# Memory features from the transposed queries, denominators from the memory's product, and one inversion of softmax sums per unit

## The chip, the core and the metric

The kernel runs on one core of a Trainium2 chip. The metric is the device time of one execution in microseconds; a median over executions is given. The engines are TensorE (PE, matrix products and, as PEld, the loading of their weights), VectorE (DVE), ScalarE (ACT), GpSimd (POOL) and SyncE (SP, which issues most DMAs). PE writes to PSUM banks; DVE and ACT read them.

## The reference

The program is a chain of three layers: attention with a compressive memory, then two feed-forward layers. Cut to what matters:

```python
B, H, S, D = 4, 8, 576, 64
local = softmax(causal(q @ k.T / sqrt(D))) @ v          # per batch and head
phi = lambda x: np.where(x > 0, x, np.exp(x) - 1.0) + 1.0
mem_ret = einsum('bhsd,bhde->bhse', phi(q), M_prev)
mem_norm = einsum('bhsd,bhd->bhs', phi(q), z_prev)[..., None] + 1e-06
g = 1 / (1 + exp(-beta))                                # per head
x = g * mem_ret / mem_norm + (1 - g) * local            # -> [2304, 512]
x = leaky_relu(x @ w1_in) @ w1_out                      # 512 -> 2048 -> 512
h = x @ w2_in
out = (h - tanh(h)) @ w2_out
```

All inputs are float64 outside the chip or float32 after a conversion that the kernel does itself: the feed-forward weights arrive as pairs of 32-bit words and are turned into float32 by integer operations on DVE.

## The kernel before, in words

**Units.** Attention is cut into 32 units, each for one batch and two heads (a pair, 128 rows of q and k transposed, 64 per head). A unit of kind A has query rows 0 to 255 (two tiles of 128) and 256 keys, a unit of kind B query rows 256 to 575 (tiles of 128, 128 and 64) and all 576 keys. The 16 A units come first, four per batch, then the 16 B units. Four units of one batch and kind give one x block of 256 rows; the 64 left-over rows of the four batches form a ninth block, R.

**A unit's work.** SP loads q and k transposed (`qk`), q once more in natural layout (`rq`), z broadcast to all partitions (`zb`), M of both heads into the diagonal blocks of a 128x128 tile (`mb`), and v. PE makes scores (L584, and L589 for the 64-row tile), DVE masks them and takes the negative maxima (L610), ACT takes the exponential with its sum (L630), DVE adds 1e-9, divides by 1-g and inverts (L637, L641: one pair of instructions per tile), the scaling of the rows goes to ACT, DVE or POOL (L647 to L651), PE transposes (L703), ACT or DVE copies out of PSUM (`e_out`), PE multiplies with v (L725) into the output bank `o`, and the result is copied to `x`.

**The memory part** runs on natural q: ACT makes relu and exp (L500, L503), DVE the features (L506) and, for each tile and head, a product with z that is summed into a denominator (L513, an instruction and the reading of its accumulator), its inverse (L519), its gate (L523) and the product with the features (L530). PE transposes the features (L547) into a score bank `s`, a copy brings them to `pT`, and one product with `mb` (L670) opens the accumulation in `o`, to which the value products add.

**The feed-forward layers.** Layer 1 works on a block of 256 rows: x is split into a high and a low part (`xs`, on ACT and DVE, L412 for the low part), 24 products per pair of weight tiles (L851, `up`), the activation and its split, 24 products down (L953). For the first four blocks it is done in two sweeps, the first with 4 of 16 weight tiles (96 products per block), the second with the rest. Layer 1's products are the filler of PE during attention. Layer 2 (L1089 to L1120) follows after all attention and layer 1. Each weight tile of layer 1 is converted in four steps on DVE (L786, L789, L794, L799) after one on ACT (L783), and split (a copy and L412).

**What sets the order.** A list scheduler in the kernel (class `Schedule`) writes each engine's instructions in a fixed order. Each piece of work has engines with costs, a priority (unit number plus an offset for loads, memory, scores, values; layer 1's PE work behind attention), tiles that it reads, writes and takes from rings (`RINGS`: three score banks `s`, two `mb`, two `qk`, one `xs`). When costs, pieces or rings change, the whole order changes. On the chip each engine runs its list in that order and waits where an operand is missing.

Of the kernel before, what the change touches and what calls it, by code (L numbers as in the profile page):

```python
# [244 lines left out]
def kernel(  # L245
# [44 lines left out]
    omg4 = const.tile([128, H // 2], F32, name="omg4")  # L290
    mbs = [const.tile([128, 128], F32, name=f"mb{i}") for i in range(RINGS["mb"])]
    gate = const.tile([128, H], F32, name="gate")
# [27 lines left out]
    nc.sync.dma_start(out=gate, in_=beta.partition_broadcast(128))  # L320
    nc.scalar.activation(out=gate, in_=gate, func=AF.Exp, scale=-1.0)
    nc.vector.tensor_scalar(out=gate, in0=gate, scalar1=1.0, scalar2=None, op0=ALU.add)
    nc.vector.reciprocal(out=gate, in_=gate)
    nc.vector.tensor_scalar(out=omg, in0=gate, scalar1=-1.0, scalar2=1.0, op0=ALU.mult, op1=ALU.add)

    nc.vector.tensor_scalar(out=omg, in0=omg, scalar1=1e-30, scalar2=None, op0=ALU.max)
    nc.vector.reciprocal(out=omg, in_=omg)
    for i in range(2):
        p = slice(64 * i, 64 * i + 64)
        nc.vector.tensor_copy(out=omg4[p], in_=omg[p].rearrange("p (h j) -> p h j", j=2)[:, :, i])  # L330
# [86 lines left out]
    class Unit:  # L417
# [14 lines left out]
        def declare(self, pr, prev):  # L432
# [15 lines left out]
            qk, rq, zb, mb, v_ = new("qk"), new("rq"), new("zb"), new("mb"), new("v" if kind == "B" else "va")  # L448
# [9 lines left out]
            def load_q(e):  # L458
                rq.tile = att.tile([128, 3, 2, 64], F32, name="rq", bufs=RINGS["rq"])
                for i, h in enumerate(heads):  # L460
                    nc.sync.dma_start(
                        out=rq.tile[:, 0:nq, i, :],
                        in_=q[b, h, q0 * 128:(q0 + nq) * 128, :].rearrange("(t p) d -> p t d", p=128))

            def load_mz(e):
                zb.tile = att.tile([128, 2, 64], F32, name="zb", bufs=RINGS["zb"])
                nc.sync.dma_start(
                    out=zb.tile.rearrange("p h d -> p (h d)"),
                    in_=z_prev[b, 2 * hp:2 * hp + 2, :].rearrange("h d -> (h d)").partition_broadcast(128))
                mb.tile = mbs[mb.seq % RINGS["mb"]]  # L470
                for i, h in enumerate(heads):
                    nc.sync.dma_start(
                        out=mb.tile[i * 64:(i + 1) * 64, i * 64:(i + 1) * 64], in_=m_prev[b, h, :, :])
# [13 lines left out]
            op([("sp", 1000)], load_q, alloc=[rq], lat=2300)  # L487
            op([("sp", 1500)], load_mz, alloc=[zb, mb], lat=2300)
# [4 lines left out]
            ph, dn = new("ph"), new("dnm")  # L493

            def flat(t):
                return t.rearrange("p t h d -> p (t h d)")[:, 0:nf]

            def phi_neg(e):
                ph.tile = att.tile([128, 3, 2, 64], F32, name="ph", bufs=RINGS["ph"])
                nc.scalar.activation(out=flat(ph.tile), in_=flat(rq.tile), func=AF.Relu, scale=-1.0)  # L500

            def phi_exp(e):
                nc.scalar.activation(out=flat(ph.tile), in_=flat(ph.tile), func=AF.Exp, scale=-1.0)  # L503

            def phi_max(e):
                nc.vector.scalar_tensor_tensor(  # L506
                    out=flat(ph.tile), in0=flat(rq.tile), scalar=1.0, in1=flat(ph.tile), op0=ALU.add, op1=ALU.max)

            def phi_den(e):
# [712 lines left out]
```

## Time and profile before

| | |
|---|---|
| median of 3 runs | 1075.63 us (1075.47 to 1076.9) |
| span of the profiled execution | 1076.9 us |
| PE busy | 1042.5 us, 97%, 7488 products |
| DVE busy | 754.0 us, 70%, 2049 instructions |
| ACT busy | 637.7 us, 59% |
| mean granted clock of TensorE | 0.989 |
| chain that ended last | PE 83%, DMA 6%, DVE 5%, ACT 4% |

The profiled execution's own time is its span, as long as the longest of the three runs. Busy times are those of the profiler: the instructions of one engine overlap at their ends, so a duration is longer than the step from one start to the next, and a busy PE is not a PE at its peak. A row of the timeline gives the start, the duration, the engine, the line, what is written and read, the shape and the count; what stands in brackets at its end is idle time before it, and who ended that. The attention units and layer 1 lie in the first 662 us or so, layer 2 in the rest.

### The profile page before, as it was taken

The page shows a single profiled execution, that of the slowest core. Times are in us where ns is not written, and L with a number is a line of the kernel's source. Part 1 is how long each engine was busy: PE and PEld are TensorE (multiplying, and loading weights), DVE is VectorE, ACT ScalarE, POOL GpSimd, SP SyncE. Part 2 cuts the span into 40 slices and gives each one's busy share as a digit, 9 for nine tenths or more (in the row PEclk, how much of TensorE's full clock was granted, in tenths as well). Part 3 has the DMA queues.
Part 4 walks back from the last instruction along what each step waited for, and adds up shares of the span by engine and source line. Part 5 has one row for each costly group of instructions (what it writes and reads, how often), then busy time and mean ns, then how long its engine had stood idle before and what let it go on. Part 6 is the DMA issues. An engine that isn't in the chain of part 4 may idle for free.

```text
span 1076.9 us, 20416 instructions
## 1 busy us (share of the span) xinstructions
PE 1042.5 (97%) x7488; PEld 918.8 (85%) x7488; DVE 754.0 (70%) x2049; ACT 637.7 (59%) x1357; POOL 100.3 (9%) x102
## 2 busy tenths in 40 slices
PE   4799999999999999999999999999999999999997
PEld 2477799778689978979999999999999999999996
DVE  6999999888677587664212366867777676777765
ACT  5889876777673277361101134766666666666664
POOL 0001000000000000000000000221222222222221
PEclk9699999999999999999999999999999999999999
DMA  7867763655644354243100055010101101010000
GB/s 223 250 177 222 225 203 107 159 153 153 183 141 137 119 165 147 89 132 102 40 2 21 10 158 186 1 41 1 40 2 39 40 1 40 1 40 20 1 20 20
DMA packets 116403, 102.52 MB, mean 95 GB/s; under 512 B 63824, under 2 KB 92496, under 8 KB 116304
## 3 DMA queue, kind: packets, MB, share of 16 engines
q1 hardware_dynamic: 115088, 99.91, 31.2%
q10 hardware_dynamic: 1216, 1.31, 0.4%
q8 instruction: 59, 0.97, 0.4%
q14 instruction: 40, 0.33, 0.1%
HBM read 78.65 MB, written 22.54 MB: 94 GB/s over the span
## 4 chain that ended last, share of the span: by engine, by line
PE 83%; DMA 6%; DVE 5%; ACT 4%; issue 1%; SPq 1%; DVEq 0%; ACTq 0%
PE up L851 36%; PE dn L1120 18%; PE dn L953 18%; PE s L703 3%; PE o L725 3%; PE s L584 3%; PE s L589 1%; PE o L670 1%; DMA cv<-in_moe_w_in_dram 1%; DMA qk<-in_qkt_dram 1%; ACT e L630 1%; DMA x2s<-g 1%; DMA w<-in_moe_w_in_dram 1%; DMA vs<-cv 1%; ACT e L647 1%
## 5 line engine op out<-in xcount | busy, mean ns | idle before, releaser
L851 PE MATMUL up<-xs,w 128*128 128x256 f32 x3456 | 454.6, 284 | 0.4 <-ACT g L930 0.4
L851 PEld LDWEIGHTS up<-xs,w 128*128 128x128 f32 x3456 | 434.1, 190 | 12.4 <-issue 5.6
L953 PE MATMUL dn<-gh,w 128*128 128x256 f32 x1152 | 160.1, 286 | 0.0
L953 PEld LDWEIGHTS dn<-gh,w 128*128 128x128 f32 x1152 | 146.0, 192 | 7.2 <-issue 6.5
L1097 DVE SCALAR_TENSOR_TENSOR gf<-u,w 128x512 f32<-128x512 f32 x72 | 85.8, 1192 | 83.4 <-ACT w L1094 83.4
L1120 PE MATMUL dn<-w,gh 128*128 128x512 f32 x568 | 143.2, 394 | 0.6 <-ACT gh L1107 0.6
L412 POOL TENSOR_TENSOR gl<-gf,gh 128x512 fp32r<-128x512 f32 x71 | 92.2, 1299 | 506.9 <-ACT gh L1107 503.3
L930 ACT ACTIVATE g<-up 128x512 f32<-128x512 f32 x72 | 42.9, 595 | 146.4 <-PE up L851 138.9
L1120 PEld LDWEIGHTS dn<-w,gh 128*128 128x128 f32 x568 | 101.6, 188 | 19.8 <-ACT gh L1107 0.8
L1089 ACT ACTIVATE u<-up 128x512 f32<-128x512 f32 x72 | 43.0, 598 | 123.7 <-PE up L851 123.7
L630 ACT ACTIVATE e<-e,mx 128x128 f32<-128x128 f32 (+4 forms) x144 | 82.7, 576 | 11.0 <-DVE mx L610 4.6
L953 PE MATMUL dn<-gl,w 128*128 128x256 f32 x576 | 84.5, 285 | 0.0
L401 DVE CAST gh<-g 128x512 fp32r<-128x512 f32 x35 | 14.9, 427 | 96.9 <-ACT g L930 96.8
L953 PEld LDWEIGHTS dn<-gl,w 128*128 128x128 f32 x576 | 75.2, 192 | 2.1 <-issue 1.9
L1120 PE MATMUL dn<-w,gl 128*128 128x512 f32 x284 | 76.2, 390 | 0.0
L610 DVE CUSTOM_DVE_ANT_0 e<-s,mask 128x128 f32<-128x128 f32 (+4 forms) x144 | 63.7, 483 | 10.6 <-PE s L584 6.6
L399 ACT ACTIVATE pt<-s 128x320 f32<-128x320 f32 (+4 forms) x149 | 58.2, 435 | 17.6 <-PE s L691 9.0
L584 PE MATMUL s<-qk 64*128 64x128 f32 (+3 forms) x256 | 53.8, 497 | 14.8 <-DMA qk<-in_qkt_dram 10.4
L703 PE MATMUL s<-identr,e 128*128 128x128 f32 x448 | 64.0, 287 | 3.9 <-ACT pT L399 2.8
L1120 PEld LDWEIGHTS dn<-w,gl 128*128 128x128 f32 x284 | 53.3, 188 | 11.9
L703 PEld LDWEIGHTS s<-identr,e 128*128 128x128 f32 x448 | 51.0, 145 | 12.9 <-ACT pT L399 3.4
L1091 DVE SCALAR_TENSOR_TENSOR hu<-up,u 128x512 f32<-128x512 f32 x72 | 49.7, 690 | 16.6 <-ACT u L1089 16.5
(105 smaller groups left out, 1334.2 us busy)
## 6 DMA issues: line engine op xcount, KB each, us to landing
w<-in_moe_w_out_dram SPq DMA_DIRECT2D x16, 512.0 KB, 5.1
cv<-in_moe_w_in_dram SPq DMA_DIRECT2D x32, 256.0 KB, 2.9
vs<-cv SPq DMA_DIRECT2D x64, 128.0 KB, 1.8
cv<-in_moe_w_out_dram SPq DMA_DIRECT2D x32, 256.0 KB, 2.9
v<-vs SPq DMA_DIRECT2D x32, 256.0 KB, 3.1
w<-in_moe_w_in_dram SPq DMA_DIRECT2D x14, 512.0 KB, 5.0
qk<-in_qkt_dram SPq DMA_DIRECT2D x16, 448.0 KB, 3.7
v<-in_v_dram SPq DMA_DIRECT2D x16, 320.0 KB, 3.5
```

What stands on the lines that cost most here:

```text
L399: nc.scalar.activation(out=out, in_=in_, func=AF.Copy)
L412: (nc.vector if e == "dve" else nc.gpsimd).tensor_tensor(out=out, in0=in_, in1=high, op=ALU.subtract)
L584: nc.tensor.matmul(ss[j].tile[:, c0:c0 + nn], lhsT=qk.tile[p, a:a + 128], rhs=qk.tile[p, kc:kc + nn], start=True, stop=True)
L610: nc.vector.tensor_tensor_reduce(out=out, in0=in0, in1=in1, scale=-scale, scalar=mx.tile[:, 0:1] if t == 4 and j else BIG, op0=ALU.add, op ...
L630: nc.scalar.activation(out=x, in_=x, func=AF.Exp, scale=-1.0, bias=mx.tile[:, k:k + 1], accum_out=sm.tile[:, j:j + 1])
L703: nc.tensor.transpose(ss[j].tile[:, a:a + 128], x, ident)
L851: nc.tensor.matmul(ps()[:, s, :], lhsT=w[:, wh * 512 + kt * 128:wh * 512 + (kt + 1) * 128], rhs=xs()[:, xh, kt, :], start=(kt == 0 and j = ...
L953: nc.tensor.matmul(dn[m // 2].tile[:, m % 2, :], lhsT=w[:, wh * 512 + m * 128:wh * 512 + (m + 1) * 128], rhs=gg.tile[:, s * 256:(s + 1) * ...
L1089: nc.scalar.activation(out=u, in_=h, func=AF.Square)
L1091: nc.vector.scalar_tensor_tensor(out=hu, in0=h, scalar=c4, in1=u, op0=ALU.mult, op1=ALU.mult)
L1097: nc.vector.scalar_tensor_tensor(out=g, in0=u, scalar=lin, in1=w, op0=ALU.mult, op1=ALU.add)
L1120: nc.tensor.matmul(dn[t], lhsT=g[:, c0:c0 + 128], rhs=w[:, wh * 512:(wh + 1) * 512], start=(p == 0 and s == 0 and j == 0), stop=(p == NP - ...
```

## The change

The memory features are now computed on the transposed q that `qk` holds anyway. They are the weights of a product with `mb`, which has two more columns holding z of either head: the product of one 128-row tile gives 128 columns of memory output and 2 denominators, into a score bank `s`. DVE adds 1e-6 and multiplies with 1/g (`ginv`, the inverse gate), inverts, and multiplies the 128 columns by the inverses while it takes them out of PSUM (`mo`). PE transposes `mo` into the output bank `o` in front of the value products; for the 64-row tile, whose memory product takes the last 128 of the 320 rows, a product with a part of the identity picks its columns. The loads of natural q and of the broadcast z go; z is loaded as a column, 64 pieces of four bytes per head. The sums of a unit's exponentials stand in one tile of five columns, so that one addition and one inversion serve the whole unit, and every scaling of the unit comes behind them. The number of `sm` buffers goes from six to three.

```diff
-    "qk": 2, "rq": 2, "xr": 1, "zb": 2, "mb": 2, "v": 1, "va": 2, "ph": 1, "dnm": 2, "pT": 1, "mx": 6, "sm": 6,
+    "qk": 2, "xr": 1, "mb": 2, "v": 1, "va": 2, "ph": 1, "dnm": 2, "mo": 1, "mx": 6, "sm": 3,
...
+                    nc.sync.dma_start(out=mb.tile[rows, i * 64:(i + 1) * 64], in_=m_prev[b, h, :, :])
+                    nc.sync.dma_start(out=mb.tile[rows, 128 + i:129 + i], in_=z_prev[b, h, :].unsqueeze(1))
...
-            op([("sp", 1000)], load_q, alloc=[rq], lat=2300)
-            op([("sp", 1500)], load_mz, alloc=[zb, mb], lat=2300)
+            op([("sp", 2000)], load_mz, alloc=[mb], lat=2300)
...
+            spans = [(min(i * 128, nqc - 128), i) for i in range(nq)]
+            def mem(e):
+                mo.tile = att.tile([128, 3, 2, 64], F32, name="mo", bufs=RINGS["mo"])
+                s.tile = s_p.tile([128, 512], F32, name="s")
+                for a, i in spans:
+                    nc.tensor.matmul(
+                        s.tile[:, i * 130:(i + 1) * 130], lhsT=ph.tile[:, a:a + 128], rhs=mb.tile,
+                        start=True, stop=True)
...
-                for i in range(nq):
-                    for j in range(2):
-                        nc.vector.tensor_tensor_reduce(
-                            out=rq.tile[:, i, j, :], in0=ph.tile[:, i, j, :], in1=zb.tile[:, j, :], scale=1.0,
-                            scalar=1e-6, op0=ALU.mult, op1=ALU.add, accum_out=dn.tile[:, i, j:j + 1])
+                nc.vector.scalar_tensor_tensor(
+                    out=dn.tile[:, 0:nq], in0=banked()[:, :, 128:130], scalar=1e-6,
+                    in1=ginv[:, 2 * hp:2 * hp + 2].unsqueeze(1).to_broadcast([128, nq, 2]),
+                    op0=ALU.add, op1=ALU.mult)
...
+            def mem_out(e):
                 nc.vector.tensor_tensor(
+                    out=mo.tile[:, 0:nq], in0=banked()[:, :, 0:128].rearrange("p t (h d) -> p t h d", h=2),
+                    in1=dn.tile[:, 0:nq].unsqueeze(3).to_broadcast([128, nq, 2, 64]), op=ALU.mult)
...
+            order["p"] = op([("pe", nq * 250 + 50)], mem, reads=[ph, mb], alloc=[s, mo], after=in_order("p"))
+            free_op([("dve", 75)], den_gate, reads=[s], alloc=[dn], port=False)
+            free_op([("dve", 110)], den_inv, reads=[dn], writes=[dn], port=False)
+            free_op([("dve", DVE(nf))], mem_out, reads=[s, dn], writes=[mo], port=False)
...
+            def sum_eps(e):
+                x = sm.tile[:, 0:sums]
+                nc.vector.scalar_tensor_tensor(
+                    out=x, in0=x, scalar=1e-9, in1=omg5[:, hp, 0:sums], op0=ALU.add, op1=ALU.mult)
...
+            def mem_tr(e):
+                o.tile = o_p.tile([128, 512], F32, name="o")
+                for a, i in spans:
+                    c, rows = i * 128, mo.tile[:, i].rearrange("p h d -> p (h d)")
+                    if a == c:
+                        nc.tensor.matmul(
+                            o.tile[:, c:c + 128], lhsT=rows, rhs=ident, is_transpose=True, start=i == 0, stop=False)
+                    else:
+                        nc.tensor.matmul(
+                            o.tile[:, c:nqc], lhsT=rows, rhs=ident[:, c - a:128], start=False, stop=False)
```

Since the scheduler sees other pieces, the order of all engines is another one. On DVE, the last rows before the second low half of the first x block (`xs<-x,xs`) read as follows in the kernel before; `dn` is the denominators, `ph` the features, `sm` the softmax sums.

```order
L641 RECIPROCAL sm<-sm 128x2
L637 SCALAR_TENSOR_TENSOR sm<-sm,omg 128x2
L519 RECIPROCAL dn<-dn 128x4
L412 TENSOR_TENSOR xs<-x,xs 128x512
L523 TENSOR_TENSOR dn<-dn,gate 128x4
L649 TENSOR_SCALAR e_650<-e_650,sm 128x128
L401 CAST xs<-x 128x512
L530 TENSOR_TENSOR ph<-ph,dn 128x256
L412 TENSOR_TENSOR xs<-x,xs 128x512
```

In the changed kernel the same place on DVE reads as follows; `e` is the masked scores of a unit's tile, `mx` its maxima.

```order
L415 TENSOR_TENSOR w_2_544<-cv,w_2_544 128x512
L787 SCALAR_TENSOR_TENSOR cv<-w_3_302,cv 128x512
L415 TENSOR_TENSOR xs<-x,xs 128x512
L592 ISA e_563,mx<-s,mask 128x128
L592 ISA mx 128x1
L592 ISA e_563,mx<-s,mask 128x128
L592 ISA mx 128x1
L592 ISA e_567,mx<-s,mask 128x256
L592 ISA mx 128x1
L592 ISA e_567,mx<-s,mask 128x256
L592 ISA mx 128x1
L415 TENSOR_TENSOR xs<-x,xs 128x512
```

The second low half is the 209th row of DVE's list before and the 124th now; all eight weight tiles that the first sweeps use were converted ahead of it before, and now five of them are.

On PE, the place where the first layer-1 products (`up`) stand read as follows before. The rows ahead are the fourth unit's value products, the sixth unit's transposes and a later unit's scores; `L670` is the fifth unit's memory product.

```order
L725 MATMUL o<-pt,va 64x256 x2
L725 MATMUL o<-pt,va 64x128 x2
L703 MATMUL s<-identr,e_567 128x128
L703 MATMUL s<-identr,e_571 128x128 x2
L703 MATMUL s<-identr,e_567 128x128
L703 MATMUL s<-identr,e_571 128x128 x2
L584 MATMUL s<-qk 128x128 x2
L584 MATMUL s<-qk 128x256 x2
L547 MATMUL s<-identr,ph 128x128 x2
L851 MATMUL up<-xs,w_0_276 128x256 x6
L670 MATMUL o<-pT,mb_69 128x256
```

Now it reads as follows; `L505` is the new memory product of the fifth unit, `L660` the transposes of a unit's memory output into `o`.

```order
L660 MATMUL o<-identr,mo 128x128 x2
L718 MATMUL o<-pt,va 64x256 x2
L718 MATMUL o<-pt,va 64x128 x2
L566 MATMUL s<-qk 128x128 x2
L566 MATMUL s<-qk 128x256 x2
L844 MATMUL up<-xs,w_0_265 128x256 x9
L696 MATMUL s<-identr,e_525 128x128
L696 MATMUL s<-identr,e_529 128x128 x2
L696 MATMUL s<-identr,e_525 128x128
L696 MATMUL s<-identr,e_529 128x128 x2
L844 MATMUL up<-xs,w_0_265 128x256 x3
L505 MATMUL s<-mb_69,ph 128x130 x2
```

The first layer-1 products stand behind the fourth unit's value products in both. Two units' transposes stood ahead of them that now stand among or behind them.

On SP the first unit's loads were q and k, two of natural q, one of z, two of M and two of v; now they are the following.

```order
L457 DMA qk<-in_qkt_dram 128x512
L465 DMA mb_69<-in_M_prev_dram 64x64
L466 DMA mb_69<-in_z_prev_dram 64x1
L465 DMA mb_69<-in_M_prev_dram 64x64
L466 DMA mb_69<-in_z_prev_dram 64x1
L475 DMA va<-in_v_dram 128x2x64 x2
L457 DMA qk<-in_qkt_dram 128x512
```

The next unit's q and k are the seventh load after the first one's, where they were the eighth.

## Rows read from the trace of the kernel before

**Rows 1.** Busy tenths of PE in 40 slices of 27 us.

```profile
PE   4799999999999999999999999999999999999997
```

**Rows 2.** Windows: us, busy of PE, PEld, DVE, ACT, POOL, clock, DMA share, GB/s.

```profile
0.00:27.00 27.00, 13.19 (x57) 8.00 (x58) 16.50 (x87) 15.78 (x45) 2.01 (x11) 0.99 0.77 224
27.00:57.00 30.00, 21.54 (x100) 12.92 (x100) 29.42 (x132) 25.54 (x78) 0.00 (x0) 0.67 0.84 251
57.00:130.00 73.00, 71.41 (x555) 56.88 (x556) 72.32 (x350) 66.58 (x199) 3.79 (x5) 1.00 0.73 206
130.00:176.00 46.00, 46.00 (x372) 43.62 (x371) 46.00 (x104) 33.10 (x65) 0.15 (x1) 1.00 0.44 144
176.00:486.00 310.00, 306.13 (x2342) 250.79 (x2341) 228.55 (x884) 186.34 (x453) 2.15 (x14) 1.00 0.51 146
```

**Rows 3.** The chain that ended last: start, us, what.

```profile
16.60 7.86 DMA w<-in_moe_w_in_dram
...
140.42 2.88 PE up L851 x24
```

**Rows 4.** Timeline of DVE, 29 to 38 us.

```profile
29.37 0.42 DVE L610 CUSTOM_DVE_ANT_0 e<-s,mask 128x256 f32<-128x256 f32 x1
29.72 0.08 DVE L610 DVE_READ_ACCUMULATOR2_ANT mx<- 128x1 f32 x1
...
34.25 0.68 DVE L799 SCALAR_TENSOR_TENSOR cv<-w,cv 128x512 int32<-128x512 int32 x1
34.85 0.22 DVE L513 CUSTOM_DVE_ANT_0 rq<-ph,zb 128x64 f32<-128x64 f32 x1
34.99 0.22 DVE L513 CUSTOM_DVE_ANT_0 rq<-ph,zb 128x64 f32<-128x64 f32 x1
...
36.70 0.16 DVE L523 TENSOR_TENSOR dn<-dn,gate 128x4 f32<-128x4 f32 x1
36.77 0.42 DVE L786 TENSOR_SCALAR cv<-cv 128x512 f32<-128x512 f32 x1
37.10 0.42 DVE L530 TENSOR_TENSOR ph<-ph,dn 128x256 f32<-128x256 f32 x1
37.44 0.69 DVE L412 TENSOR_TENSOR w<-cv,w 128x512 fp32r<-128x512 f32 x1
```

**Rows 5.** Timeline of DVE and PE, four places.

```profile
55.45 0.69 DVE L412 TENSOR_TENSOR xs<-x,xs 128x512 fp32r<-128x512 f32 x1
56.28 0.51 PE L851 MATMUL up<-xs,w 128*128 128x256 f32 x3
128.76 0.87 PE L725 MATMUL o<-pt,va 128*64 128x256 f32 x8
174.29 0.69 DVE L412 TENSOR_TENSOR w<-cv,w 128x512 fp32r<-128x512 f32 x1
```

**Rows 6.** Timeline of PE, 132 us and 236 to 242 us.

```profile
132.80 0.27 PE L691 MATMUL s<-identr,e 128*128 128x128 f32 x1
...
236.76 0.95 PE L851 MATMUL up<-xs,w 128*128 128x256 f32 x6
237.64 2.28 PE L725 MATMUL o<-pt,v 128*64 128x320 f32 x20
239.85 1.13 PE L584 MATMUL s<-qk 64*128 64x512 f32 x4
240.91 0.81 PE L670 MATMUL o<-pT,mb 128*128 128x320 f32 x2
...
241.78 0.49 PE L547 MATMUL s<-identr,ph 128*128 128x128 f32 x3
```

**Rows 7.** DMA issues: count, KB each, median us to landing.

```profile
rq<-in_q_dram SPq DMA_DIRECT2D x32, 64.0 KB, 2.7
zb<-in_z_prev_dram SPq DMA_DIRECT2D x32, 64.0 KB, 4.0
mb<-in_M_prev_dram SPq DMA_DIRECT2D x64, 16.0 KB, 3.2
```

**Rows 8.** Timeline of SP's queue, 11 us.

```profile
11.35 1.11 SPq L472 DMA_DIRECT2D mb<-in_M_prev_dram  x2
```

More of the change, by code (lines that the diff above doesn't have):

```diff
@@ L289 @@
     mask4 = const.tile([128, S // 2], BF16, name="mask4")
-    omg4 = const.tile([128, H // 2], F32, name="omg4")
-    mbs = [const.tile([128, 128], F32, name=f"mb{i}") for i in range(RINGS["mb"])]
-    gate = const.tile([128, H], F32, name="gate")
+    omg5 = const.tile([128, H // 2, 5], F32, name="omg5")
+    mbs = [const.tile([128, 130], F32, name=f"mb{i}") for i in range(RINGS["mb"])]
+    ginv = const.tile([128, H], F32, name="ginv")
     omg = const.tile([128, H], F32, name="omg")
@@ L319 @@
     nc.vector.memset(thr_t, -T2)
[L320 to L324, printed above, removed]
+    nc.sync.dma_start(out=ginv, in_=beta.partition_broadcast(128))
+    nc.scalar.activation(out=ginv, in_=ginv, func=AF.Exp, scale=-1.0)
+    nc.vector.tensor_scalar(out=ginv, in0=ginv, scalar1=1.0, scalar2=None, op0=ALU.add)
+    nc.vector.reciprocal(out=omg, in_=ginv)
+    nc.vector.tensor_scalar(out=omg, in0=omg, scalar1=-1.0, scalar2=1.0, op0=ALU.mult, op1=ALU.add)
     nc.vector.tensor_scalar(out=omg, in0=omg, scalar1=1e-30, scalar2=None, op0=ALU.max)
     nc.vector.reciprocal(out=omg, in_=omg)
+    pairs = omg.rearrange("p (h j) -> p h j", j=2)
+    for i in range(2):
+        nc.vector.tensor_copy(out=omg5[:, :, 2 * i:2 * i + 2], in_=pairs)
     for i in range(2):
         p = slice(64 * i, 64 * i + 64)
-        nc.vector.tensor_copy(out=omg4[p], in_=omg[p].rearrange("p (h j) -> p h j", j=2)[:, :, i])
+        nc.vector.tensor_copy(out=omg5[p, :, 4], in_=pairs[p, :, i])
     wt = [[None] * NF for m in range(2)]
@@ L445, in in_order @@
                 return [prev.order[name]] if prev else []
-            qk, rq, zb, mb, v_ = new("qk"), new("rq"), new("zb"), new("mb"), new("v" if kind == "B" else "va")
+            qk, mb, v_ = new("qk"), new("mb"), new("v" if kind == "B" else "va")
             n0 = 0 if kind == "A" else NA
@@ L541, in declare @@
-            s, pT = new("s"), new("pT")
-            def tr_p(e, s=s):
-                pT.tile = att.tile([128, 320], F32, name="pT", bufs=RINGS["pT"])
-                s.tile = s_p.tile([128, 512], F32, name="s")
-                for i in range(nq):
-                    nc.tensor.transpose(
-                        s.tile[:, i * 128:(i + 1) * 128], ph.tile[:, i].rearrange("p h d -> p (h d)"), ident)
-            def p_out(e, s=s):
-                copy(e, pT.tile[:, 0:nqc], s.tile[:, 0:nqc])
@@ L553, in declare @@
-            order["p"] = op([("pe", nq * 109 + 50)], tr_p, reads=[ph], alloc=[s, pT], after=in_order("p"))
-            free_op(copies(nqc, True), p_out, reads=[s], writes=[pT], port=False)
+                    out=mo.tile[:, 0:nq], in0=banked()[:, :, 0:128].rearrange("p t (h d) -> p t h d", h=2),
+                    in1=dn.tile[:, 0:nq].unsqueeze(3).to_broadcast([128, nq, 2, 64]), op=ALU.mult)
+            op([("act", ACT(nqc))], phi_neg, reads=[qk], alloc=[ph])
+            op([("act", ACT(nqc))], phi_exp, reads=[ph], writes=[ph])
@@ L559, in declare @@
             made = {}
+            sm = new("sm")
+            sums = 2 * nq - (kind == "B")
             for tiles in ([[0, 1]] if kind == "A" else [[2], [3], [4]]):
```

96 lines of the change are left out of this document (34 added, 62 removed).

## The prediction

> **What bounds the kernel now.** I read the slices of the page first. TensorE (PE) is busy in nine tenths or more of every slice from the third on, but only in four and seven tenths of the first two [rows 1]. [...] So from 57 us on PE is the bound, and what is left to win there is PE work itself. Ahead of it somebody else is the bound: VectorE (DVE) is busy 29.4 of 30 us in 27 to 57, 72.3 of 73 in 57 to 130, and 46.0 of 46 up to 176 [rows 2]. DVE converts the first layer's weights there and does the softmax and the memory features of the 16 A units; the first 27 us, where DVE has 16.5, belong to transfers: a pair of weight tiles takes 7.86 us to land there, on the chain that ended last [rows 3], with the DMA engines 0.77 to 0.84 busy at 224 to 251 GB/s [rows 2].
>
> How DVE paces the start can be summed. I price each DVE row of the built order with its start-to-start time, since neighbours overlap: 0.60 us for a 512-column two-operand step, 0.34 for 256 columns, 0.145 for one denominator product (two at 34.85 and 34.99), 0.07 to 0.09 for the small ones [rows 4]. All rows up to the second low half of the first x block, the last thing that the first up product waits for, make 43.7 us; the row ends at 56.1 (55.45 + 0.69) and the product starts at 56.28 [rows 5]. So DVE lost 12.4 us by then. Up to the last converted weight the rows make 160.5 us and it ends at 175.0 [rows 5]: 14.5 lost, 2 of them in 119 us. DVE's queue is the clock of this stage.
>
> PE's side: 24 up products take 2.88 us, 0.12 each [rows 3]. A 128-column transpose costs 0.11 ((0.49 - 0.27) / 2, from three and from one). After six up products of 0.12 (from 236.76) the next form of the array starts at 237.64 and not at 237.48, and about as much again goes on the first load: I take 0.2 us per change of form. The value products x20 stream 2432 columns (six passes of 320, two of 192, two of 64, both heads at once) from 237.64 to the next form's start at 239.85, less that 0.2: 0.83 ns a column and pass [rows 6]. By these prices PE's rows up to the sixteenth unit's value products are 90.0 us; they end at 129.6 (128.76 + 0.87) [rows 5]. PE idles 39.6 us in that stretch, and little later.
>
> **The change part by part.** *Denominators.* 160 products with their accumulator reads go from DVE: 4 x 0.145 = 0.58 us per A unit, 0.87 per B unit, 9.3 us over the A units [rows 4]. What replaces them, one addition-and-gate of 4 or 6 columns, was there before as the gate's own instruction.
>
> *Softmax sums.* An A unit has one pair of small instructions where it had two, a B unit one for three: 48 pairs less, about 0.15 us each, 2.4 us over the A units.
>
> *The pass through PSUM.* The copy of the transposed features goes; the product with 1/denominator stays on DVE but reads PSUM. The nearest row that reads PSUM, a maximum of 256 columns, takes 0.34 to 0.35 us from start to start (29.37 to 29.72), against 0.34 for the product from SBUF (37.10 to 37.44) [rows 4]; I take no difference. [...]
>
> *Feature functions.* They take 256 columns as before in an A unit, 320 in place of 384 in a B unit: under 0.1 us each on DVE and ScalarE, off the path.
>
> *Sum for DVE.* Rows up to the second x half: 29.5 us, 14.2 less, of which 6.5 are conversions that the new order puts later. Up to the last weight: 147.6, 12.9 less.
>
> *PE.* The transposes of the features (80 x 0.11 = 8.8 us) become 64 transposes into the output bank (7.0) and 16 short products (two passes at 0.11, 3.5). The memory product was 16 of 256 and 16 of 320 columns, two passes: 15.3 us at 0.83 ns a column. It becomes 80 products of 130 columns with the features as weights. A pass streams 0.108 us; no row shows full-height float32 weights of 128 columns changed at every pass of so few. From below it is 0.11 (the transposes change weights each time and hide the load), from above 0.22 (load and stream one after the other, as the first pass after a change of form does). I take 0.11, the nearest row: 17.6 us. The order has 164 changes of form where there were 175, -2.2. Sum: (7.0 + 3.5 - 8.8) + (17.6 - 15.3) - 2.2 = +1.8 us of PE work, none of it hidden, PE being the bound. The upper end would be 17.6 more.
>
> *Transfers.* The q loads go: 64 DMAs of 64 or 96 KB, and zb, 64 KB each [rows 7]. Per A unit that is 2 x 64 + 64 KB less, 768 KB for the four units of the first x block; at some 240 GB/s, between the two rates of the start [rows 2], 3 us. In its place two z loads of 64 four-byte pieces stand behind M on SP's queue, where an M load takes 0.58 us to issue (1.11 for two at 11.35 [rows 8]), and whatever stands behind them there (v, the next q and k, weights) waits that much; the two q issues are gone from that place. I take DVE's loss as 11.5 us in place of 12.4, between no relief and the 3 us.
>
> **The sum.** First up product: 29.5 + 11.5 = 41 us, some 15 earlier. That is not the gain. An x block of an A group feeds 96 matmuls until the later weights are converted, and in the new order PE has used up the first block's 96 before the eighth unit's value products; only 3 come before the ninth's. So PE waits for DVE again, and what counts is when DVE lets the A units go. DVE's rows up to the sixteenth unit's inverse are 95.8 us (104.8 before); at 107.3 it is done, and scaling, six transposes (0.7), copies and the value products (0.87 [rows 5]) follow, with their hand-overs an estimated 4.3 us: 111.6. PE's rows up to there are 78.0, so 33.6 us idle in place of 39.6: -6.0. From there on PE always has layer-1 work in both orders, and idles as before. -6.0 + 1.8 = -4.2. The profiled execution has a span of 1076.9 us, as long as the longest of the runs shown and 1.3 over their median: 1072.7 in its terms, 1071.4 against the median of 1075.6. I say 1071.5, own range 1068 to 1075.
>
> **The rivals.** *The start's full relief.* Were PE fed from 41 us on without a gap, the whole 14.2 us of queue would come back: -14.2 + 1.8, 1063. For it speaks that DVE's loss after 57 us is only 2 us in 119; against it the 96 matmuls of a block.
>
> *Nothing arrives.* With DVE's loss at 14 or more in the new order, because its rows now wait for PE in the middle of a unit (the memory product stands between phi and the product with 1/denominator), and ScalarE, 66.6 of 73 us busy [rows 2], as the next bound, idle falls by 2 only: 1075.
>
> *Slower: memory operands hold PE's queue.* The memory product stands in PE's own queue ahead of the next unit's scores, and it needs M and the four-byte z, which land last. M takes 3.2 us in the median to land and zb 4.0 [rows 7]. If each A unit's product waits 0.6 us, one more issue, that is 9.6 us, PE and DVE both standing: 1081. It decides where PE reaches the product before z has landed. [...]
>
> *Slower: loads in the open.* At 0.22 a pass, 1071.5 + 17.6 = 1089. Against it: the second pass of the old product starts with its load already done (0.81 us for two passes of 320 columns, where two loads of 0.11 in the open would make it 0.92 [rows 6]).
>
> **How the numbers follow.** A measurement of this kernel can tell about 0.2% (2.2 us) from no change: "same" is 1073.5 to 1077.8. Forecast 0.46, of which 0.38 lie below that band and 0.08 in it; full relief 0.16, faster; nothing arrives 0.18, of which 0.02 faster, 0.13 same, 0.03 slower; memory operands 0.13 and open loads 0.07, slower. Together faster 0.56, same 0.21, slower 0.23. The range goes from 1062 to 1081: it takes in the full relief and the held queue and leaves out the open loads.
>
> **What would show it.** Right: the first up product at 39 to 44 us; PE short of work between about 60 and 110 us with DVE still nine tenths busy; the sixteenth unit's value products ending near 112; the last weight converted near 160; the memory product at 0.11 us a pass and PE full after 115 us. Wrong: memory products with idle ahead that a z or M transfer ends; passes of 0.2 us; DVE below nine tenths before 110 us, which would put the bound on ScalarE or on transfers; or new idle on PE after 176 us, where B units now hold their score banks and wait for a whole unit's sums.

## The result and the profile after

The changed kernel takes 1086.1 us (median of 4, 1084.4 to 1087.5) against 1075.9 of the kernel before (1075.5 to 1076.9) in the same comparison: ratio 1.0086, 95% interval 1.0074 to 1.0099. It is slower by 10 us where I had forecast 4 us faster, and outside my range.

The slices of after first, PE and the clock:

```profile
PE   5789999989999999999999999999999999999997
...
PEclk9889999999999999999999999999999999999999
```

The first slice is a tenth fuller than before, but the third and the ninth have 8 where before had 9 [rows 1], and the clock, which before was lowest in the second slice (0.67 from 27 to 57 us [rows 2]), has a dip in the second and third. The windows, same columns as [rows 2]:

```profile
0.00:27.00 27.00, 14.91 (x76) 9.65 (x76) 18.53 (x77) 16.60 (x49) 1.98 (x11) 1.00 0.69 215
27.00:57.00 30.00, 23.43 (x150) 17.25 (x150) 27.94 (x98) 24.63 (x72) 0.00 (x0) 0.89 0.74 215
57.00:130.00 73.00, 67.60 (x527) 54.05 (x526) 70.46 (x251) 66.46 (x195) 2.06 (x4) 0.95 0.69 215
130.00:176.00 46.00, 45.22 (x366) 41.18 (x364) 41.49 (x99) 32.51 (x66) 0.15 (x1) 1.00 0.32 103
176.00:486.00 310.00, 301.13 (x2317) 250.18 (x2313) 203.97 (x610) 163.80 (x406) 2.12 (x14) 0.99 0.42 128
```

PE gains 3.6 us of busy time up to 57 us and loses 3.8 from 57 to 130 and 5.0 from 176 to 486, although VectorE has 25 us less to do in the last of them (204.0 for 228.6 [rows 2]). So from 176 us on PE now waits in a stretch in which no engine is full. The landmarks, against [rows 5]:

```profile
39.73 0.39 PE L844 MATMUL up<-xs,w 128*128 128x256 f32 x1
41.60 0.69 DVE L415 TENSOR_TENSOR xs<-x,xs 128x512 fp32r<-128x512 f32 x1
111.89 0.42 DVE L524 TENSOR_TENSOR mo<-s,dn 128x256 f32<-128x256 f32 x1
112.23 0.17 DVE L628 RECIPROCAL sm<-sm 128x4 f32<-128x4 f32 x1
117.26 0.87 PE L718 MATMUL o<-pt,va 128*64 128x256 f32 x8
163.97 0.70 DVE L415 TENSOR_TENSOR w<-cv,w 128x512 fp32r<-128x512 f32 x1
213.45 0.83 PE L505 MATMUL s<-mb,ph 128*128 128x130 f32 x6
```

The first up product comes at 39.7 us, the second low half of the first x block ends at 42.3 (56.1), the sixteenth unit's value products end at 118.1 (129.6), the last weight is converted at 164.7 (175.0). In before the first up product came at 55.84; the row at 56.28 in [rows 5] is the fourth of six, of which its window shows the last three:

```profile
55.84 0.95 PE L851 MATMUL up<-xs,w 128*128 128x256 f32 x6
```

The sixteenth unit's sums are inverted at 112.2, no earlier than in before, where its inverse starts at 111.16. There the unit's memory features came last, and the value products waited for them:

```profile
111.16 0.17 DVE L641 RECIPROCAL sm<-sm 128x2 f32<-128x2 f32 x1
...
126.31 0.42 DVE L530 TENSOR_TENSOR ph<-ph,dn 128x256 f32<-128x256 f32 x1
...
128.23 0.60 PE L670 MATMUL o<-pT,mb 128*128 128x256 f32 x2
```

So what the change took away in the A stage is that last wait for the memory features: 18.5 us passed from the inverse to the end of the value products, and 5.9 pass now.

To place PE's idle I take the step from each product's start to the next, less what it streams (0.119 us for 256 columns of layer 1, 0.109 for a transpose, 0.83 ns a column and pass for the rest) and 0.206 per change of form (in [rows 6] 0.09 ahead of the first product, 237.55 to 237.64, and 0.11 on it: of the two at 240.91 the first takes 0.37 to the next, 0.27 of it streaming). This idle is larger than the profile's own, whose ends are modelled. By it, before and after: up to the sixteenth unit 37.1 and 39.9 us (23.9 and 24.1 by the profile's own idle, so the 2.8 us more are not shown); from there to the last unit's value products ("B stage" below) 5.5 and 16.6, of which 4.3 and 13.8 stand ahead of the transposes of the scaled exponentials. Those transposes in the list of groups, 130 to 490 us, of before and then of after (busy us, mean ns, idle before them by the profile's count):

```profile
L703 PE MATMUL s<-identr,e 128*128 128x128 f32 x341 | 44.8, 277 | 0.8 <-ACT pt L399 0.6
```

```profile
L696 PE MATMUL s<-identr,e 128*128 128x128 f32 x316 | 44.1, 284 | 8.1 <-ACT pt L402 6.5 <-DVE e L642 0.8
```

They wait for ScalarE's copies `pt` of the transposes ahead of them, which empty the three score banks. Two such places in after, ACT and PE; the first stands behind a weight load:

```profile
173.03 0.43 ACT L776 ACTIVATE cv<-cv 128x256 f32<-128x256 f32 x1 [1.68 <-DMA cv<-in_moe_w_in_dram]
173.36 1.49 ACT L402 ACTIVATE pt<-s 128x320 f32<-128x320 f32 x4
...
173.83 0.88 PE L696 MATMUL s<-identr,e 128*128 128x128 f32 x6 [0.78 <-ACT pt L402]
```

The second is the longest:

```profile
235.25 1.23 ACT L640 ACTIVATE e<-e,sm 128x384 f32<-128x384 f32 x2 [0.67 <-DVE sm L628]
235.81 1.72 PE L696 MATMUL s<-identr,e 128*128 128x128 f32 x9 [0.85 <-DVE e L642]
237.62 1.09 ACT L923 ACTIVATE g<-up 128x512 f32<-128x512 f32 x2 [1.15 <-DMA x2s<-g]
238.59 0.47 ACT L490 ACTIVATE ph<-qk 128x320 f32<-128x320 f32 x1
238.95 0.63 ACT L402 ACTIVATE gh<-g 128x512 fp32r<-128x512 f32 x1
239.47 0.77 ACT L402 ACTIVATE pt<-s 128x320 f32<-128x320 f32 x2
239.96 1.33 PE L696 MATMUL s<-identr,e 128*128 128x128 f32 x5 [2.44 <-ACT pt L402]
```

ScalarE had nothing to do from 236.5, stood 1.15 us for a store (`x2s<-g`) that had to free its tile, did four other pieces, and only then the copies; PE idled 2.44 us. PE's granted clock was 0.50 for the 6.8 us from 239.3, as it had been for 6.8 us from 75.4 on, behind a gap of 1.64 us that ended at 74.93; before had no such stretch from 54 us to the end of its products. The windows of these two stretches, the later one first:

```profile
239.30:246.10 6.80, 6.14 (x24) 4.65 (x25) 3.94 (x13) 4.57 (x13) 0.15 (x1) 0.50 0.30 89
...
75.40:82.20 6.80, 5.89 (x30) 4.23 (x29) 6.37 (x23) 5.47 (x14) 0.00 (x0) 0.50 0.68 211
```

PE is busy 6.14 and 5.89 us there with products that the prices above put at 3.3 and 3.1, so by this estimate the lower clock cost some 3 us each time, besides the gaps.

What ScalarE waited for from 130 to 490 us (us, times, longest), loads only, of before and then of after:

```profile
ACT cv L783 <- DMA cv<-in_moe_w_out_dram: 15.2, 10, 4.0
ACT cv L783 <- DMA cv<-in_moe_w_in_dram: 8.0, 8, 2.7
```

```profile
ACT cv L776 <- DMA cv<-in_moe_w_in_dram: 22.4, 15, 4.0
ACT cv L776 <- DMA cv<-in_moe_w_out_dram: 13.0, 8, 3.8
ACT ph L490 <- DMA qk<-in_qkt_dram: 2.4, 4, 0.8
```

23.2 us on loads before, 37.8 after (stores, `x2s<-g`: 2.3 and 1.3). ScalarE has time for them; the copies queued behind do not. Of the eight longest waits of after ahead of those transposes, four have a wait for a load ahead of the copies in ScalarE's queue (at 174, 189, 407 and 423 us). Of the others one has the store shown above, two have other work of ScalarE (259 and 292 us), and one waits for VectorE (235.8 us).

### The profile page after: what moved, and what is told of

Its sections match the earlier page's. It is cut to its first block, busy times and chain, and to the rows that moved or that the text cites. A ratio compares the mean times of both kernels' runs of the same rounds, so it can differ in the third digit from the quotient of the medians.

```text
span 1085.7 us, 20126 instructions
## 1 busy us (share of the span) xinstructions
PE 1046.3 (96%) x7600; PEld 927.0 (85%) x7600; DVE 727.0 (67%) x1638; ACT 621.4 (57%) x1323; POOL 98.3 (9%) x101
## 4 chain that ended last, share of the span: by engine, by line
PE 76%; DVE 7%; ACT 7%; DMA 7%; issue 2%; SPq 1%; POOL 0%; ACTq 0%; DVEq 0%; POOLq 0%
PE up L844 32%; PE dn L1113 18%; PE dn L946 15%; PE o L718 3%; DMA qk<-in_qkt_dram 3%; PE s L696 3%; PE s L566 2%; ACT e L612 2%; ACT e L640 1%; DVE e L592 1%; PE s L505 1%; DVE cv L792 1%; PE s L571 1%; DMA w<-in_moe_w_out_dram 1%; DMA cv<-in_moe_w_in_dram 1%
## 5 line engine op out<-in xcount | busy, mean ns | idle before, releaser
L844 PE MATMUL up<-xs,w 128*128 128x256 f32 x3456 | 448.6, 284 | 3.2 <-DVE xs L415 1.2
L404 DVE CAST gh<-g 128x512 fp32r<-128x512 f32 x42 | 17.9, 427 | 108.8 <-ACT g L923 108.7
L1093 DVE COPY_PREDICATED gf<-mk,up 128x512 f32<-128x512 int32 x72 | 53.9, 748 | 7.7 <-DVE up L1092 0.5
```

The costliest lines, as they stand in the source:

```text
L844: nc.tensor.matmul(ps()[:, s, :], lhsT=w[:, wh * 512 + kt * 128:wh * 512 + (kt + 1) * 128], rhs=xs()[:, xh, kt, :], start=(kt == 0 and j = ...
L1093: nc.vector.copy_predicated(out=g, mask=mk.bitcast(I32), data=h)
```

## The experiments

The table comes first, since the runs are read together. "Ratio" is to the kernel before in the same comparison (three rounds, 4 to 10 runs). "To A" is PE's idle up to the sixteenth unit, "tr" that ahead of the transposes in the B stage, both by my count above ("to A" adds up some 700 priced steps: 3 ns of error in one price are 2 us, so small differences in it carry no weight); "loads" is what ScalarE waited for weight, q and k loads from 130 to 490 us; "layer 2" is the start of its first output product.

| kernel | ratio (95%) | to A | tr | loads | layer 2 |
|---|---|---|---|---|---|
| before | 1 | 37.1 | 4.3 | 23.2 | 672.5 |
| after | 1.0086 (1.0074-1.0099) | 39.9 | 13.8 | 37.8 | 684.4 |
| e1_mem | 1.0095 (1.0068-1.0122) | 36.3 | 13.2 | 51.8 | 683.5 |
| e2_sums | 1.0041 (1.0026-1.0056) | 41.3 | 4.6 | 34.9 | 682.5 |
| p_before | 0.998 (0.997-0.999) | 35.8 | 3.4 | 24.6 | 669.8 |
| p_after | 1.0012 (0.9997-1.0027) | 37.9 | 12.0 | 50.2 | 677.4 |
| q2 | 1.0073 (1.005-1.0097) | 42.0 | 11.1 | 40.4 | 685.4 |
| q2p | 1.01 (1.0084-1.0117) | 36.1 | 14.9 | 42.1 | 685.6 |
| mirror | 1.0315 (1.03-1.033) | 60.5 | 9.0 | 39.5 | 707.0 |
| lat | 1.0048 (1.0031-1.0065) | 37.4 | 7.7 | 46.0 | 679.4 |
| s_before | 1.0004 (0.9995-1.0013) | 35.4 | 4.0 | 4.9 | 671.6 |
| s_after | 1.0001 (0.9992-1.0011) | 37.7 | 3.4 | 6.9 | 673.9 |
| d_before | 1.0003 (0.9993-1.0012) | 36.7 | 6.1 | 0 | 672.0 |
| d_after | 0.9992 (0.9982-1.0002) | 37.9 | 6.4 | 1.2 | 672.1 |
| x_sbefore | 1.0014 (1.0004-1.0024) | 41.1 | 3.8 | 9.2 | 674.0 |
| x_safter | 0.9968 (0.9953-0.9982) | 33.1 | 3.2 | 13.3 | 672.5 |
| ds_after | 1.0003 (0.999-1.0015) | 39.2 | 3.4 | 0 | 674.6 |
| p_ds | 0.9965 (0.9952-0.9978) | 38.1 | 4.4 | 0 | 671.1 |
| s_e1 | 0.9939 (0.9924-0.9954) | 34.5 | 5.0 | 5.4 | 667.5 |
| s_e2 | 0.9989 (0.9978-0.9999) | 46.4 | 3.1 | 7.2 | 678.5 |

### One part at a time: e1_mem and e2_sums

e1_mem is after, with the sums by tile again (and six `sm` buffers); e2_sums is before, with the sums by unit (and three). The additions, inversions and scalings move with them; the cut shows only where the tile is made.

```
-            sm = new("sm")              # e1_mem, from after
+                ei, sm = et[i], new("sm")
...
-                ei, sm = et[i], new("sm")   # e2_sums, from before
+            sm = new("sm")
```

> Kernel after with each query tile's softmax sums inverted apart again, as before; the memory part stays new. Theory 1 (the wait for a whole unit's sums holds the B units' transposes in TensorE's queue; in the trace of after TensorE idles 12.6 us ahead of the transposes in the B stage, before 3.2): the 9.4 us go, 1076.7 us, transposes' waits in the B stage 3 to 4 us. Theory 2 (the memory part makes the waits, by the slots it needs between phi and the scaling): 1084 to 1087, waits as in after. Theory 3 (any other list of pieces is dealt in another order, and the differences of 5 to 10 us come from the order): anywhere from 1072 to 1088, with waits at other places.

> Kernel before with a unit's softmax sums inverted together, as after; the memory part stays old. Theory 1: 1075.9 + 9.4 = 1085 us, with 10 us or more of waits ahead of the transposes in the B stage. Theory 2: 1074 to 1077. Theory 3: anywhere from 1072 to 1088.

Theory 1, which I held first, falls for the B stage. With the old sums the transposes idle 13.2 us as in after; with the new sums alone 4.6 as in before. The wait came in with the memory part. The list of groups of e1_mem, the transposes from 130 to 490 us:

```profile
L689 PE MATMUL s<-identr,e 128*128 128x128 f32 x325 | 44.1, 281 | 6.0 <-ACT pt L402 5.3 <-DVE e L629 0.4
```

e2_sums loses in another place: 4.2 us more idle than before up to the sixteenth unit. It also shows that ScalarE's waits alone don't hold the transposes: it stands 34.9 us for loads, nearly as long as after, with 4.6 us of idle there.

### The order alone: p_before and p_after

```
-    ("pe", "act"): 197, ("pe", "dve"): 197,
+    ("pe", "act"): 207, ("pe", "dve"): 207,
```

> Kernel before with one number of the planner changed: it reckons 207 ns in place of 197 between a TensorE product and its reader on ScalarE or VectorE. The same pieces of work, dealt in another order. Theories 1 and 2: the kernel's time is a property of its pieces, 1074 to 1078 us. Theory 3: off from 1075.9 by 4 us or more.

> Kernel after with the same number of the planner changed (207 ns in place of 197). Theories 1 and 2: 1084 to 1088 us. Theory 3: off from 1086.1 by 4 us or more.

Ten nanoseconds in the scheduler's plan move after by 8 us (1.0086 to 1.0012) and before by 2. Theory 3 holds in part: a single order of this kernel is known no better than that, and a time alone can't name a cause. But the transposes' idle stays 12.0 in p_after and 3.4 in p_before: that is a mark of the kind of kernel, and I went by it from here. The ratio of p_after also flatters it: up to layer 2 it is 7.6 us behind p_before, and layer 2, 2.8 us shorter in it, gives some of that back (last section).

### What stands in front of the copies: q2, q2p, mirror, lat

In 6 of the 8 longest waits of after, feature functions of the next unit stood in front of the copies. They read the q and k load now, and start where it lands. q2 gives them a load of their own (q2p: the same with 207), mirror ties the old features to the q and k load, lat tells the plan alone that this load takes 5 us.

```
+        in_=qkt[b, 2 * hp:2 * hp + 2, :, n0 + qc:n0 + qc + nqc]...    # q2, into "rq", 2 buffers
-                    out=ph.tile[:, 0:nqc], in_=qk.tile[:, qc:qc + nqc], func=AF.Relu, scale=-1.0)
+                    out=ph.tile[:, 0:nqc], in_=rq.tile[:, 0:nqc], func=AF.Relu, scale=-1.0)
...
-            op([("act", ACT(nf))], phi_neg, reads=[rq], alloc=[ph])   # mirror, in before
+            op([("act", ACT(nf))], phi_neg, reads=[rq, qk], alloc=[ph])
...
-            op([("sp", 600)], load_qk, alloc=[qk], lat=3000)          # lat, in after
+            op([("sp", 600)], load_qk, alloc=[qk], lat=5000)
```

> Kernel after, with the transposed queries for the feature functions loaded a second time into a ring of their own (as the untransposed ones were before), so that features no longer wait for the unit's large q and k load. Theory 4 (features now start where that load lands, in the middle of the unit ahead, and stand in ScalarE's queue in front of the copies for which TensorE's transposes wait; in after 6 of the 8 longest waits ahead of transposes in the B stage have them there): TensorE's idle ahead of transposes in the B stage falls from 13.8 us to 4 to 6, the time to 1076 to 1079. Theory 1 (the grouped sums make those waits): idle stays at 12 or more, 1085 to 1087. Theory 3 (order alone): the idle goes up or down by some us with the features not in front of the copies in either case.

> The kernel with the second load of the transposed queries, and the planner's 207 ns in place of 197 between TensorE and its readers: another order of the same pieces. Theory 4: the idle ahead of transposes stays at 4 to 6 us in this order too, 1072 to 1079. Theory 3: off by 4 us or more from the kernel with 197, with the idle ahead of transposes no nearer to that of before.

> Kernel before, with one dependency added: a unit's features wait for its large q and k load, though they read their own. No other edit. Theory 4: idle ahead of transposes in the B stage rises from 4.3 us to 9 or more, with feature functions in front of the copies; the time to 1080 to 1084. Theory 3: 1072 to 1080, with idle of 3 to 5 there. Theory 2 (the memory product and its slots): no change, 1075 to 1077.

> Kernel after; the planner alone is told that the q and k load takes 5 us in place of 3 (it takes 3.6 in the median). Theory 4: features are dealt behind the landing, ScalarE's waits for the load (4.7 us in after) go, half or more of the idle ahead of transposes in the B stage stays, since features still come in the middle of the unit: 1078 to 1084. Theory 3: anywhere in 1074 to 1090.

q2 and q2p refute theory 4 as I had put it: the features are out of the way, the transposes still idle 11.1 and 14.9 us. The timeline of q2, ACT and PE at one of the places, shows what took their stead:

```profile
211.32 1.14 PE L703 MATMUL s<-identr,e 128*128 128x128 f32 x9
212.91 0.43 ACT L783 ACTIVATE cv<-cv 128x256 f32<-128x256 f32 x1 [1.60 <-DMA cv<-in_moe_w_out_dram]
213.25 1.07 ACT L402 ACTIVATE pt<-s 128x320 f32<-128x320 f32 x3
213.72 0.55 PE L703 MATMUL s<-identr,e 128*128 128x128 f32 x3 [1.26 <-ACT pt L402]
```

It is the first step of a layer-2 weight conversion, and it waits for its load; the seven longest waits of q2 ahead of transposes all have that step right in front of the copies, six of them with a wait for its load. So not the features alone matter, but any ScalarE piece that the plan puts at a load's landing: theory 5. mirror loses 34 us where 4 to 8 were expected, most of it (23 us of idle) in the A stage, so tying features to the large load is dear by itself. Its rise in the B stage to 9.0 is the size expected, but weight loads (39.5 us for 23.2) and not the q and k load are what its ScalarE stands for there, so it does not show theory 4. lat halves the idle (7.7), though ScalarE's waits on loads rise to 46.0; the conversions' loads stand in front of its two longest waits.

### Later loads in the plan, or the step off ScalarE: s_after, s_before, d_after, d_before

```
-            op([("sp", 600)], load_qk, alloc=[qk], lat=3000)          # s_after, s_before
+            op([("sp", 600)], load_qk, alloc=[qk], lat=5000)
-            op([("sp", 500)], load, alloc=[raw], lat=2600, after=after)
+            op([("sp", 500)], load, alloc=[raw], lat=2600 if layer == 0 else 4600, after=after)
...
+            nc.vector.tensor_scalar(                                  # d_after, d_before, layer 2
+                out=gi(), in0=words(1), scalar1=0x7FFFFFFF, scalar2=None, op0=ALU.bitwise_and)
```

> Kernel after; the planner alone is told that the q and k load and the second layer's weight loads land 2 us later than it reckoned (5 and 4.6 us in place of 3 and 2.6). Theory 5 (the list was dealt with loads that land later on the chip than in the plan; ScalarE then waits for a load, 37.8 us of such waits from 130 to 490 us in after and 23.2 in before, and the copies behind it hold the transposes): those waits fall below 20 us, the idle ahead of transposes in the B stage below 5, the time to 1074 to 1079. Theory 4 (only the features in front of the copies): idle 6 to 9 as with the q and k load alone, 1081 to 1084. Theory 3: no relation between the waits and the time.

> Kernel before with the same two numbers of the planner. Theory 5: the waits on loads fall here too (from 23 us to 15 or less), but they cost little here (idle ahead of transposes 4.3 us), so 1073 to 1077. Theory 3: 1070 to 1084.

> Kernel after; the first step of a second-layer weight conversion, the one that waits for its load, goes from ScalarE to VectorE (64 steps of some 0.35 us). ScalarE then can't stand for a weight load with the copies behind it. Theory 5: idle ahead of transposes in the B stage 3 to 7 us in place of 13.8, 1076 to 1081. Theory 4: it stays at 10 or more, as the features stay in front, 1084 to 1088. VectorE has some 70 us to spare from 176 to 486 us, so the added 22 us cost nothing by themselves unless VectorE now stands for the loads with maxima behind it.

> Kernel before with the same step on VectorE. Theory 5: little to win (idle ahead of transposes 4.3 us), and VectorE, fuller here, now stands for the loads: 1074 to 1080. If the step's place matters in the same way in both kernels, the difference after minus before falls below 4 us.

Theory 5 holds in all four. In s_after ScalarE's waits on loads fall from 37.8 to 6.9 us, the transposes' idle from 13.8 to 3.4, the ratio from 1.0086 to 1.0001; the same two numbers do nothing for before, though its waits fall to 4.9. So the loss is gone, but the change as a whole still gains nothing: s_after reaches layer 2 2.3 us behind s_before. The waits of s_after on loads, and its transposes:

```profile
ACT cv L776 <- DMA cv<-in_moe_w_out_dram: 4.5, 1, 4.5
...
ACT cv L776 <- DMA cv<-in_moe_w_in_dram: 2.4, 2, 2.1
```

```profile
L696 PE MATMUL s<-identr,e 128*128 128x128 f32 x352 | 44.9, 278 | 0.2
```

d_after reaches the same time by another way, by which ScalarE can't stand for a layer-2 weight load at all; 6.4 us of the idle stay, as in d_before (6.1). VectorE, which takes the step over, stood idle 106 us of the 310 from 176 on in after, more than the 70 I had named. Why do the loads hurt after and not before? Shown is that after's ScalarE stands at them longer, and in part with copies behind. Standing longer is not enough (e2_sums: 34.9 us of waits, 4.6 of idle), so it is what the order puts behind them, and why the memory part brings such orders stays open. That the 25 us freed on VectorE let the plan run load, conversion and store closer together is my reading of it, and was not tried.

### Whether VectorE paces the start: x_sbefore, x_safter; both cures: ds_after, p_ds

```
-        op([("dve", DVE(n / 2))], c_max, reads=[g], writes=[g])      # x_sbefore, x_safter
+        if layer:
+            op([("dve", DVE(n / 2))], c_max, reads=[g], writes=[g])
```

x_sbefore and x_safter are s_before and s_after without the lower bound on the magnitude in every first-layer conversion. ds_after is s_after with the step of d_after; p_ds is ds_after with 207.

> Kernel before with the later loads in the plan (1077.5 us), less one VectorE step of every first-layer conversion, the lower bound on the magnitude (32 steps of 0.34 us, 10.9 us of VectorE's queue up to the last weight; what is left out is that bound). If VectorE's queue is what TensorE waits for up to the end of the A stage, as the prediction has it (9 us less rows up to the sixteenth unit gave 6 us less idle), two thirds of the part that stands ahead of the sixteenth unit (about 15 steps, 5 us) come back: 1073 to 1075. If TensorE's idle there is set by what it is given to do (layer-1 products per converted weight, transfers of the first 27 us), 1076 to 1079.

> The same step left out of kernel after with the later loads in the plan (1077.3 us). VectorE as the pace: some 18 steps, 6 us, stand ahead of the sixteenth unit, 1072 to 1075. Otherwise 1076 to 1079.

> Kernel after with both cures: the two loads 2 us later in the plan, and the second layer's first conversion step on VectorE. Theory 5: both take away the same waits, so they don't add up: 1073 to 1077, idle ahead of transposes in the B stage 3 to 6 us. If they were two causes, 1067 to 1071.

> The kernel with both cures in another order (207 ns in place of 197 between TensorE and its readers in the plan). Theory 5: with the waits gone the order decides less than it did in after (7 us): within 3 us of the other, 1072 to 1079.

11 us less on VectorE made the order of before no faster (idle up to the sixteenth unit 41.1 for 35.4), and that of after 3.5 us faster (33.1 for 37.7). Inconclusive as to size, since each is dealt anew; but it speaks against VectorE's work turning into PE's time at two thirds in the kernel before. The cures don't add up (ds_after 1.0003), as theory 5 had it. p_ds came out 4 us from ds_after, not within 3: the order still decides that much.

### The parts again with later loads: s_e1 and s_e2

e1_mem and e2_sums with the two numbers of s_after.

> The memory part alone (softmax sums apart as before; 1.0095 of before, 13.2 us idle ahead of transposes in the B stage, ScalarE's waits on loads 52 us there), with the two loads 2 us later in the plan. Theory 5: waits below 20 us, idle 3 to 5 us, 8 to 10 us less time, a ratio to before of 0.999 to 1.002. Theory 3: any ratio from 0.996 to 1.010, with no relation to the waits.

> The sums alone (1.0041 of before, idle ahead of transposes in the B stage only 4.6 us, 4 us more idle than before up to the sixteenth unit), with the two loads 2 us later in the plan. Theory 5: its loss isn't that of the loads in the B stage, so 0 to 2 us of it go, a ratio of 1.002 to 1.005. If the later loads help whatever the loss is, 0.999 to 1.001.

s_e1 is the best of all: 1071.1 us, 0.9939 (0.9924 to 0.9954), 17 us from e1_mem by two numbers of a plan, where 8 to 10 were expected. It beats both kernels; 2.8 us of its lead over before are the shorter layer 2 (last section). Its windows, same columns as [rows 2]:

```profile
57.00:130.00 73.00, 70.14 (x565) 57.42 (x565) 70.76 (x268) 69.15 (x201) 3.49 (x8) 1.00 0.70 208
...
176.00:486.00 310.00, 307.10 (x2413) 258.38 (x2412) 204.22 (x653) 165.06 (x411) 2.78 (x14) 1.00 0.43 126
```

s_e2 has 11 us more idle up to the sixteenth unit than s_before by my count (4.2 more by the profile's own), and its ratio, 0.9989, is better than expected only because layer 2 itself is 7 us shorter in it (last section). Up to layer 2, where nothing of that counts, the four kernels with later loads give the parts: memory 671.6 to 667.5 (-4.1), sums 671.6 to 678.5 (+6.9), and sums on top of memory 667.5 to 673.9 (+6.4). With the loads as they were, the sums cost 10.0 us up to layer 2 on before and 0.9 on e1_mem. Each is one order of its kernel, and two orders lay up to 8 us apart. In the four pairs (before and e2_sums, e1_mem and after, both with later loads) the grouped sums add idle up to the sixteenth unit by my count: 4.2, 3.6, 11.0 and 3.2 us; by the profile's own idle 1.1, -2.3, 4.2 and 5.0, so in the second pair it is not shown. A cause would be theory 1 in the A stage: a unit's first scaling waits for its fourth exponential, and from the fourth exponential to the unit's first transpose it takes 0.2 to 0.7 us longer in each pair (mean of the last 12 units, e1_mem 4.04, after 4.76). But single units lie between 3.2 and 8.4 us in after, so this is a hint and no proof.

## Why the prediction was wrong, point by point

- **The start.** Right as a mechanism, but the 41 us forecast for the first up product met the 39.7 measured by luck. It was worked out for the end of the second low half, which ended at 42.3: by the prediction's own count (time less priced rows) VectorE lost 12.8 us up to there and not 11.5, so the relief by fewer transfers hardly came (by the profile VectorE stood idle 10.4 us up to there, 11.1 in before). The first up product waits for no second low half: in before it started at 55.84, ahead of the half's end at 56.13, and in after the eighth is the first to wait for it, at 42.34.
- **"At 107.3 it is done ... 111.6": failed by size.** The inverse came at 112.2, so VectorE's loss by the prediction's own count was 16.4 us and not 11.5 (it stood idle 13.1; its rows were busy 99.1 against 95.8 priced). From the inverse to the end of the value products it was 5.9 us and not 4.3. 118.1 in place of 111.6: with PE's rows at 78.0 its idle is 40.1 by the prediction's own count, against 39.6. The -6.0 was +0.5. The comparison behind it, rows of 95.8 against 104.8 before, took too late a row in before: the sixteenth unit's inverse stood at 111.16 there, with 99.6 us of VectorE busy up to its end, and what held the value products was the memory features at 126.31.
- **"From there on PE always has layer-1 work in both orders, and idles as before": failed, and this decided.** PE had the work, but its queue is in order, and the transposes at its head waited for ScalarE's copies: +11.1 us of idle in the B stage, 9.5 of them ahead of those transposes. With the loads planned later this goes (13.8 to 3.4 in s_after), with the conversion's first step off ScalarE most of it does (6.4 in d_after). I had put "new idle on PE after 176 us" on the list of what would prove me wrong, for the grouped sums; the place was right and the cause wrong. I had looked at ScalarE's share (186 of 310 us [rows 2]) and not at what stands first in its queue.
- **What the sums do.** I priced them as 2.4 us less of VectorE and gave the delay of the scaling no price. Up to layer 2 they cost 6 to 7 us with later loads, 10.0 and 0.9 with the loads as they were, in one order each.
- **PE's work.** Right: the memory product takes 0.111 us a pass (the six at 213.45: 0.83 less the last one's 0.28, over five steps), 164 changes, no load in the open. Reading PSUM cost no more, as I had taken it: the product from the bank takes 0.34 us from start to start (111.89 to 112.23), as from SBUF [rows 4].
- **The rivals.** "Memory operands hold PE's queue" had the right sign for a wrong reason: PE waited once for z, 3.5 us at the start. The DMA issues show M and z landing alike:

```profile
mb<-in_M_prev_dram SPq DMA_DIRECT2D x64, 16.0 KB, 2.3
mb<-in_z_prev_dram SPq DMA_DIRECT2D x64, 0.2 KB, 2.3
```

"Loads in the open" didn't happen.
- **The account.** From after's trace against before's: idle to the sixteenth unit +2.8, B stage +11.1, layer 2 -2.7, the rest (work, layer 1's end) -2: +9.2 at PE's last product (1071.8 and 1081.0). The split between the first two is no better than the count; the rest is what is left over. That the memory part alone, with its loads planned late, gives -4.1 up to layer 2 (s_before to s_e1) does not bear out the forecast of -4.2: it is one order of each kernel, ds_after and p_ds are 4 us apart, and the forecast was for both parts.

## What to carry to other kernels

An engine that is half busy (ScalarE in after, 163.8 of the 310 us from 176 on) can still set the pace where its queue is in order: look at what it waits for and what stands behind the waiting instruction, above all at instructions that begin where a transfer lands. When a change frees an engine in a kernel whose order a scheduler writes, plan the loads with room again before judging the change; here two latencies in the plan were worth 9 to 17 us in the kernels with the new memory part (after and e1_mem), more than the change, and nothing in the kernel before. And one order is one sample: deal a second one before a difference of some microseconds is put down to an edit.

## What had not been expected of the hardware

Layer 2's output and up products, 2520 in the same sequence in the five traces compared (before, p_before, after, e2_sums, s_e1), take different times by kernel, evenly over the whole stretch. First and last output product of before, after and e2_sums:

```profile
672.50 0.51 PE L1120 MATMUL dn<-w,gh 128*128 128x512 f32 x1 [0.62 <-ACT gh L1107]
...
1071.55 0.61 PE L1133 MATMUL dn<-w,gl 128*128 128x512 f32 x2
```

```profile
684.44 0.50 PE L1113 MATMUL dn<-w,gh 128*128 128x512 f32 x1
...
1080.76 0.61 PE L1126 MATMUL dn<-w,gl 128*128 128x512 f32 x2
```

```profile
682.48 0.50 PE L1130 MATMUL dn<-w,gh 128*128 128x512 f32 x1 [0.53 <-ACT gh L1117]
...
1074.62 0.61 PE L1143 MATMUL dn<-w,gl 128*128 128x512 f32 x2
```

399.1, 396.3 and 392.1 us; the same in every reordered kernel of a kind (399.3 from the first start to the last in before, p_before and s_before, 396.5 or 396.6 in after, e1_mem, s_after, s_e1 and p_ds, 392.4 in e2_sums and s_e2). A 256-column product takes 120.2, 118.7 and 117.8 ns on average in the stretch behind attention. By the diff the kinds differ there only in the tiles that they declare. But e1_mem and q2, which declare other tiles than after, take the same 118.7 ns as after, so the place of tiles is a guess that was not tried, and the cause stays open. It is a term of 3 to 7 us that neither the diff nor the order shows.
